# An attention kernel's last six exps made whole again, its jitter seeds redrawn

## The chip, the cores and the metric

One core of one Trainium2 chip runs the whole program. The metric is the device time of one execution in microseconds, the median over several runs. The profile is of one execution, and times inside it count from its first instruction.

## What is computed

The input `x` has 2,048 rows of 512 values. It is layer-normalised; the result feeds multi-query attention with 32 heads of 16 (one key and one value head) and a dense branch with a hidden width of 1,792; the two are multiplied and added to `x`.

```python
def _A_ref(x, wq, wk, wv, wo):
    B, S, D = x.shape
    H = 32
    Dh = D // H
    q = (lambda x, *d: x.transpose(*d))((x @ wq).reshape(B, S, H, Dh), 0, 2, 1, 3)
    k = x @ wk
    v = x @ wv
    scores = jnp.einsum("bhqd,bkd->bhqk", q, k) * (Dh ** -0.5)
    p = _softmax(scores, axis=-1)
    o = jnp.einsum("bhqk,bkd->bhqd", p, v)
    return (lambda x, *d: x.transpose(*d))(o, 0, 2, 1, 3).reshape(B, S, H * Dh) @ wo

def _B_ref(x, w1, w2):
    h = jnp.einsum("bsd,df->bsf", x, w1)
    h = _silu(h)
    out = jnp.einsum("bsf,fd->bsd", h, w2)
    return out

x = A_x
xn = _layernorm(x, axis=-1)
s = _A_ref(xn, A_wq, A_wk, A_wv, A_wo)
g = _silu(_B_ref(xn, B_w1, B_w2))
return x + s * g
```

## The kernel before

**Tiles.** Queries come in four chunks of 512 (`NQ`), heads in octets; a *group* is one chunk with the even or the odd heads of an octet, four heads in four row strips of TensorE, and there are `NG` = 32 groups. A group has 64 *scores*: four heads by sixteen key tiles of 128, each a matmul of 32 x 128 weights with 512 columns into one PSUM bank (L866). Seven banks (`BANKS`) serve scores and jobs, the eighth (`OB`) collects a group's products with V.

**Two ways to exponentiate.** Most scores go to ScalarE, which takes the exp of up to three banks in one instruction (L1717, into `pa_sb`). The others go to VectorE in *batches* of four, one for each head: one `tensor_scalar` writes a 16-bit pattern that reads as an approximate exponential (L1002, into `db_sb`), and three more copies of the whole batch with an integer added (`ds_sb`, "shifts") are made by GpSimd (L1202) or VectorE (L1196). Four such copies with four weighted versions of V make the approximation, so a VectorE score (a "D slot") costs four PV matmuls and a ScalarE score one. PV matmuls run as rounds of up to four, side by side in four column strips (L1282). `END_DV` lets VectorE take shifts in the last group once fewer than that many of its scores are left; `MARGIN_END` is the number of scores that must be left in the last group for a new batch to start (`d_batch`).

**Jobs.** Rounds of the projections and of the dense branch (`q`, `h`, `z`, `w`; L511) fill TensorE between score phases.

**The order.** No order is written by hand. A planner (`Planner`, and the `*_step` functions) walks through modelled time at build time, always for the engine that is furthest behind, and appends what that engine does next; semaphore waits come from the dependences. The order on each engine is then fixed. `do_S` places a *score phase* of up to four scores and decides how many go to VectorE: with four free banks two, with three one, or two when fewer than about ten PV matmuls are queued for the two open groups (`held`: a job holds a bank; Q3 = QUEUE = 10, Q4 = -1, J3 = N3 = 1, J4 = N4 = 2). A backlog of VectorE tasks (`dve_backlog`, which counts a shift only while `END_DV` lets VectorE take it) lowers this to one or none:

```python
queue = sum(len(q) for g in range(st["gO"], min(st["gO"] + 2, NG)) for q in pvq[g])
...
if held:
    want = J4 + (queue < vary(Q4)) if n == 4 else J3 + (queue < vary(Q3))
else:
    want = N4 if n == 4 else max(N3, 2 * (queue < vary(QUEUE)))
```

`vary` multiplies a threshold by a random factor of width `SPREAD`; the generator gets the next of `SEEDS` every `STRETCH` = 64 phases.

**The end.** When at most `RH` = 6 ScalarE scores are left, `begin_halves` and `half_step` take their exps by halves of 256 queries (L1667), first all first halves, then all second halves. PV rounds follow by halves, and `last_norm` is called once for each half: transpose of the PV sums (`f_sb`, L1306), reciprocal (L1309), multiplication (L1311), transpose back (`on_sb`, L1316). `make_tail` sets up the output projection of the last four row tiles (four `wo` rounds each, the last of which needs `on_sb`), as soon as no job is left (`MT_EARLY`). `scaled` multiplies its result by the gate: for row tiles 0 and 2 (`EVR`) ScalarE copies the bank to SBUF (L714) and VectorE multiplies from there (L716); tiles 1 and 3 are multiplied straight from PSUM (L719). Tiles 0 to 2 are added to `x` by TensorE (L1503) and copied out by ScalarE (L1508), tile 3 by VectorE (L731). SyncE issues the stores (L725).

Of the kernel before, what the change touches and what calls it, by code (L numbers as in the profile page):

```python
# [15 lines left out]
P = 128  # L16
DH = 16
# [4 lines left out]
SEEDS, STRETCH, SPREAD = (2502, 4652, 1398, 4134, 3319, 6151, 8548, 1413, 942, 5642), 64, 0.3  # L22
# [30 lines left out]
MARGIN, MARGIN_END = 16, 20  # L53
# [15 lines left out]
END_DV = 40  # L69
RH, EVR, SC_PRIO, MT_EARLY = 6, (0, 2), 0, 1  # L70
# [225 lines left out]
def bass_recurrent_scan__grouped_kv_mqa__dense_activation_silu__prompt_kernel(  # L296
# [30 lines left out]
    with ExitStack() as es:  # L327
# [383 lines left out]
        def scaled(tt, b, r=None):  # L711
            k = tt % 2
            if r in EVR:
                ev = pl.add(Task(AC, 490.0, lambda a: a.activation(xn_sb[:, r, :], bank(b), ACT.Copy, scale=0.25),  # L714
                                 [("ps", b)], [("xn", r)], 0))
                fin_task[tt] = Task(DV, 333.0, lambda v: v.tensor_tensor(fin_sb[:, k, :], xn_sb[:, r, :], tmp_sb[:, tt % 8, :], ALU.mult),  # L716
                                    [("xn", r), ("tmp", tt % 8)], [("fin", k)], SC_PRIO, [ev, tmp_task[tt], fin_task.get(tt - 2)], ports=2)
                return fin_task[tt]
            fin_task[tt] = Task(DV, T_P, lambda v: v.scalar_tensor_tensor(  # L719
                out=fin_sb[:, k, :], in0=bank(b), scalar=0.25, in1=tmp_sb[:, tt % 8, :], op0=ALU.mult, op1=ALU.mult),  # L720
                [("ps", b), ("tmp", tt % 8)], [("fin", k)], 0 if r is None else SC_PRIO, [tmp_task[tt], fin_task.get(tt - 2)])
            return fin_task[tt]
# [92 lines left out]
        st = dict(half=0, halfdone=False, half1=[0] * 4, gA=0, gD=0, gO=0, fill=0, expn=0, assigned=0)  # L815
# [179 lines left out]
        def pass_d(b, bt, g, i, kt):  # L995
            tot[g, i] += K

            def placed(pop):
                pool_free.append(b)
                pvq[g][i].append((pop, v_lhs(1, g, kt), db_sb[:, bt.b, i * NQ:(i + 1) * NQ].bitcast(BF16),  # L1000
                                  [("Db", bt.b, i)] + v_reads(1, kt), ("d", bt), None))
            bt.P[i] = pl.add(Task(DV, T_P, lambda v: v.tensor_scalar(  # L1002
                db_sb[:, bt.b, i * NQ:(i + 1) * NQ], bank(b), 128.0 * LOG2E, 128.0 * (SHIFT_BETA + 127.0),
                op0=ALU.mult, op1=ALU.add), [("ps", b)], [("Db", bt.b, i)], 0, on_place=placed))
# [163 lines left out]
        def split(bt, s, j):  # L1168
# [3 lines left out]
            def ready(pop, slots):  # L1172
                for i in slots:
# [3 lines left out]
                                         [("Ds", s, i)] + v_reads(j, kt), ("s", s), None))  # L1177
# [38 lines left out]
        def pv_round(t):  # L1216
# [9 lines left out]
            liked = "a" if ap >= PA_HI else "s" if ap <= DS_HI and all(ds_busy) else "ads"  # L1226
            soon, old = INF, INF
            for half in ((None, 0, 1) if st["half"] else (None,)):
                got = {}
                if half == 1 and (st["half"] < 2 or last_t1[0].op is None):  # L1230
                    break
                for i in range(4):
                    pick = None
                    for k, ent in enumerate(pvq[g][i]):
                        if ent[5] != half:
                            continue
                        if v_task.get(ent[3][-1][2]) is None or v_task[ent[3][-1][2]].op is None:
                            continue
                        r = max(pl.vis(ent[0], PE), pl.ready(PE, ent[3], ()))
                        if r <= t + 20:  # L1240
                            key = (ent[4][0] not in liked, k)
                            if pick is None or key < pick[0]:
                                pick = (key, k, r)
                            if key[0] is False:
                                break
                            continue
                        if pick is None:
                            soon = min(soon, r)
                    if pick is not None:
                        got[i] = pick[1]  # L1250
                        old = min(old, pick[2])
                if got:
                    break
# [6 lines left out]
        def do_pv(t, got):  # L1260
# [3 lines left out]
            for i in sorted(got):  # L1264
                ent = pvq[g][i].pop(got[i])
                op_, lhs, rhs, rd, rel, half = ent
# [10 lines left out]
            cols = slice(0, NQ) if half is None else slice(half * NQ // 2, (half + 1) * NQ // 2)  # L1277

            def emit(pe, mm=tuple(mm)):
                h = None  # L1280
                for (i, lhs, rhs, s0, s1) in mm:
                    h = pe.matmul(bank(OB)[32 * i:32 * (i + 1), cols], lhsT=lhs, rhs=rhs, start=s0, stop=s1,  # L1282
                                  tile_position=(0, 32 * i), skip_group_check=True)
                return h
            pl.place(PE, MM if half is None else MM / 2, emit, sorted(reads, key=str), [("ps", OB)], t0=max(t, pe_start(pl.clk[PE], "C")))
            pl.set_mode("C")
            make_shifts()
            if st["half"] == 1 and not any(e[5] != 1 for q in pvq[g] for e in q) and st["halfdone"] and all(
                    tot[g, i] - done[g, i] == st["half1"][i] for i in range(4)):
                last_norm(g, 0)  # L1290
# [4 lines left out]
        def last_norm(g, h):  # L1295
            oi, e = divmod(g, 2)
            k = g % 2
            f3 = f_sb[:, k, :].rearrange("p (b d) -> p b d", d=32)
            o3 = otr_sb[:, oi % 2, :].rearrange("p (b d) -> p b d", d=32)
            den = DH if e == 0 else 0  # L1300
            val = 0 if e == 0 else DH
            nb = NQ // 64
            cols = slice(h * NQ // 2, (h + 1) * NQ // 2)
            bl = slice(h * nb, (h + 1) * nb)
            late = last_t1[-1:] if h else [norm.get(("m", g - 2))]
            t1 = pl.add(Task(DV, 0.5 * T_TR + 30.0, lambda v: v.transpose(f_sb[:, k, cols], bank(OB)[:, cols]),  # L1306
                             [("ps", OB)], [("F", k, h)] + [("F", k)] * (h == 0), 1 + h, late))
            last_t1.append(t1)
            t2 = pl.add(Task(DV, 110.0, lambda v: v.reciprocal(rcp_sb[:, k, bl], f3[:, bl, den]),  # L1309
                             [("F", k, h)], [("rcp", k, h)], 3, [t1]))  # L1310
            t3 = pl.add(Task(DV, 200.0, lambda v: v.tensor_tensor(  # L1311
                o3[:, bl, val:val + DH], f3[:, bl, val:val + DH],
                rcp_sb[:, k, bl].unsqueeze(2).to_broadcast([P, nb, DH]), ALU.mult),
                [("F", k, h), ("rcp", k, h)], [("otr", oi % 2, 1, h)] + [("otr", oi % 2, 1)] * (h == 0), 3,
                [t2, t2_task.get(oi - 2)], ports=2))
            last_on.append(pl.add(Task(DV, 0.5 * T_TR + 30.0, lambda v: v.transpose(  # L1316
                on_sb[:, oi % NON, cols], otr_sb[:, oi % 2, cols]),
                [("otr", oi % 2, 0), ("otr", oi % 2, 1, h)], [("on", oi % NON, h)] + [("on", oi % NON)] * (h == 0), 4 + h,
                [t3, norm[("m", g - 1)]] + last_on)))
            if h:  # L1320
                norm[g] = t1
            st["half"] = 2 + h

        last_t1 = []
        last_on = []

        def make_norm(g):
# [6 lines left out]
            if g == NG - 1:  # L1334
                for h in range(len(last_t1), 2):
                    last_norm(g, h)
                return
# [112 lines left out]
        tb = []  # L1450
        tail = dict(made=False, items=[], sums=[])

        def make_tail():
            tail["made"] = True
            c = NC - 1
            free = sorted((pl.ready(PE, (), [("ps", b)]), b) for b in pool_free)
            held = [u.bank for u in units[st["expn"]:]]
            tb.extend([b for _, b in free] + held)
            assert sorted(tb) == list(BANKS), tb
            for r in range(4):  # L1460
                tt = 4 * c + r
                for o in range(NOC):
                    def emit(pe, r=r, o=o):
                        return col4(pe, tb[r], lambda j: on_sb[:, (NOC * c + o) % NON, r * P + 32 * j:r * P + 32 * (j + 1)],
# [9 lines left out]
        def tail_round(t):  # L1474
            soon = INF
            for n, (_, r, o, emit) in enumerate(tail["items"][:1]):
# [5 lines left out]
                rr = pl.ready(PE, tail_reads(r, o), [("ps", tb[r])]) if tb[r] in pool_free else INF  # L1482
# [3 lines left out]
            for n, (r, part) in enumerate(tail["sums"]):  # L1486
# [5 lines left out]
                rr = pl.ready(PE, [("fin", tt % 2)] if part else [("xr", tt % 4)], () if part else [("ps", tb[4 + r])]) if tb[4 + r] in pool_free else INF  # L1492
# [5 lines left out]
        def do_tail(t, it):  # L1498
            if it[0] == "s":
# [3 lines left out]
                pl.place(PE, MM, lambda pe: pe.matmul(bank(tb[4 + r]), lhsT=ident[:, :], rhs=src, start=part == 0, stop=part == 1),  # L1503
                         [("fin", tt % 2) if part else ("xr", tt % 4)] + [("id", i) for i in range(4)], [("ps", tb[4 + r])],
                         t0=max(t, pe_start(pl.clk[PE], "F")))
                pl.set_mode("F")
                if part:
                    t2 = pl.add(Task(AC, 490.0, lambda a: a.activation(ob_sb[:, tt % 4, :], bank(tb[4 + r]), ACT.Copy),  # L1508
                                     [("ps", tb[4 + r])], [("ob", tt % 4)], 0, [out_task.get(tt - 4)]))
# [3 lines left out]
            pl.place(PE, MM, emit, tail_reads(r, o), [("ps", tb[r])], t0=max(t, pe_start(pl.clk[PE], "C")))  # L1513
            pl.set_mode("C")
            if o == NOC - 1:
                tt = 4 * (NC - 1) + r
                if r < 3:
                    stt[r] = pl.add(scaled(tt, tb[r], r))
                else:
                    for tk in final(tt, tb[r]):  # L1520
# [299 lines left out]
```

## Time and profile before

| what | value |
|---|---|
| median of 4 runs | 669.73 us (669.61 to 670.07) |
| the profiled execution | 670.07 us |
| its span, first to last instruction | 668.3 us |
| busy: PE, ACT, DVE, POOL | 98%, 98%, 92%, 84% |
| score matmuls; to VectorE | 2,048; 736 |
| shifts by GpSimd; by VectorE | 544; 8 |
| exps by ScalarE, whole; by halves | 671; 6 |

PE is TensorE's matmuls, PEld its weight loads, DVE VectorE, ACT ScalarE, POOL GpSimd and SP SyncE. L1282 is line 1282 of the kernel; a line of the timeline gives the start and the duration in us, engine, line, operation, output and input, how many, and in brackets the idle time before and what ended it. A matmul's own duration is longer than the time that it keeps TensorE from the next one, so costs are taken from starts.

### The profile page before, as it was taken

How to read it: one execution, taken by the hardware profiler on the slowest of the kernel's cores; microseconds unless marked ns; L12 is line 12 of the kernel's file. 1: busy time of each engine (PE TensorE's matmuls, PEld its weight loads, DVE VectorE, ACT ScalarE, POOL GpSimd, SP SyncE). 2: the span in 40 equal slices, each digit the busy share in tenths (PEclk: the TensorE clock that was granted, in tenths of full speed). 3: DMA queues.
4: the chain of work that ended last, by engine and by line, in shares of the span. 5: the costliest groups of instructions: out<-in, count | busy, mean ns of one | idle time of the engine just before them, and what ended most of it. 6: DMA issues, size and time to landing. Idle time of an engine off the chain costs nothing.

```text
span 668.3 us, 21224 instructions
## 1 busy us (share of the span) xinstructions
PE 656.9 (98%) x8963; PEld 190.9 (29%) x8963; DVE 614.9 (92%) x1093; ACT 652.0 (98%) x768; POOL 558.8 (84%) x556
## 2 busy tenths in 40 slices
PE   7999999999999999999999999999999999999997
PEld 4422222222222222222222222222222222222223
DVE  8989999899989998999998999999899999998995
ACT  6999999999999999999999999999999999999996
POOL 3049889989898899898899887999899989998972
PEclk9999999999999999999999999999999999999999
DMA  9500000000000000000000000000000000000000
GB/s 292 174 9 2 2 2 2 2 3 1 2 2 18 19 18 18 1 2 2 2 2 2 17 18 18 18 2 1 3 2 2 2 18 17 18 18 2 2 2 33
DMA packets 11821, 12.86 MB, mean 19 GB/s; under 512 B 1808, under 2 KB 11216, under 8 KB 11728
## 3 DMA queue, kind: packets, MB, share of 16 engines
q1 hardware_dynamic: 10928, 10.78, 5.1%
q8 instruction: 72, 1.18, 0.8%
q10 hardware_dynamic: 800, 0.72, 0.3%
q14 instruction: 21, 0.17, 0.1%
HBM read 8.95 MB, written 2.10 MB: 17 GB/s over the span
## 4 chain that ended last, share of the span: by engine, by line
PE 75%; ACT 17%; DVE 5%; DMA 1%; issue 0%; SPq 0%; ACTq 0%
PE ps L1282 33%; PE ps L866 25%; PE ps L511 17%; ACT pa_sb L1717 16%; DVE db_sb L1002 1%; ACT t_sb L669 1%; DVE stats_sb L458 1%; DMA ds_sb<-in_A_x_dram 1%; DVE u_sb L671 1%; DVE xn_sb L487 0%; DVE xnT_sb L538 0%; SPq L393 0%; DVE fin_sb L719 0%; DVE kt_sb L567 0%; DVE mv_sb L462 0%
## 5 line engine op out<-in xcount | busy, mean ns | idle before, releaser
L1202 POOL INT64_ADD ds_sb<-db_sb x544 | 553.1, 1038 | 91.8 <-DVE db_sb L1002 35.2
L1717 ACT ACTIVATE pa_sb<-ps 128x1024 bf16<-128x1024 f32 (+2 forms) x671 | 616.3, 1029 | 5.8 <-PE ps L866 3.4
L1002 DVE TENSOR_SCALAR db_sb<-ps 128x512 uint16<-128x512 f32 x736 | 475.0, 682 | 39.8 <-PE ps L866 28.9
L1282 PE MATMUL ps<-ds_sb,v_sb 128*32 128x512 bf16 x2208 | 274.4, 383 | 0.0
L866 PE MATMUL ps<-qt_sb,kt_sb 32*128 32x512 bf16 x2048 | 250.7, 384 | 3.7 <-ACT pa_sb L1717 1.1
L1282 PE MATMUL ps<-pa_sb,v_sb 128*32 128x512 bf16 x1317 | 245.8, 382 | 0.0
L1282 PE MATMUL ps<-db_sb,v_sb 128*32 128x512 bf16 x736 | 176.2, 383 | 0.0
L866 PEld LDWEIGHTS ps<-qt_sb,kt_sb 32*128 32x128 bf16 x2048 | 62.6, 90 | 275.5 <-ACT pa_sb L1717 154.5
L1282 PEld LDWEIGHTS ps<-ds_sb,v_sb 128*32 128x32 bf16 x2208 | 68.4, 95 | 60.4 <-issue 41.9
L511 PE MATMUL ps<-xnT_sb,w_sb 128*32 128x512 bf16 x896 | 72.0, 384 | 0.0
L1282 PEld LDWEIGHTS ps<-pa_sb,v_sb 128*32 128x32 bf16 x1317 | 60.7, 95 | 39.3 <-issue 26.7
L511 PE MATMUL ps<-w_sb,u_sb 128*32 128x512 bf16 x820 | 64.2, 384 | 0.0
L1282 PEld LDWEIGHTS ps<-db_sb,v_sb 128*32 128x32 bf16 x736 | 43.7, 95 | 20.3 <-issue 15.9
L669 ACT ACTIVATE t_sb<-ps 128x512 bf16<-128x512 f32 x72 | 45.2, 628 | 0.0
L671 DVE SCALAR_TENSOR_TENSOR u_sb<-t_sb,ps 128x512 bf16<-128x512 bf16 x56 | 38.3, 684 | 1.4
L618 PE MATMUL ps<-w_sb,u_sb 32*128 32x512 bf16 x76 | 29.2, 384 | 0.0
L511 PEld LDWEIGHTS ps<-xnT_sb,w_sb 128*32 128x32 bf16 x896 | 17.2, 94 | 27.3 <-issue 21.5
L511 PEld LDWEIGHTS ps<-w_sb,u_sb 128*32 128x32 bf16 x820 | 15.4, 95 | 23.0 <-issue 19.7
L1338 DVE STREAM_TRANSPOSE f_sb<-ps 128x512 f32<-128x512 f32 x31 | 21.9, 706 | 0.1
L511 PE MATMUL ps<-wo_sb,on_sb 128*32 128x512 bf16 x256 | 19.8, 383 | 0.0
L511 PE MATMUL ps<-xnT_sb,wq_sb 128*32 128x512 bf16 x240 | 18.8, 384 | 0.0
L1342 DVE TENSOR_TENSOR otr_sb<-f_sb,rcp_sb 128x256 bf16<-128x256 f32 x31 | 12.9, 416 | 1.4 <-POOL ds_sb L1202 1.1
(75 smaller groups left out, 167.7 us busy)
## 6 DMA issues: line engine op xcount, KB each, us to landing
w_sb<-in_B_w_dram SPq DMA_DIRECT2D x2, 1792.0 KB, 14.4
xr_sb<-in_A_x_dram SPq DMA_DIRECT2D x16, 128.0 KB, 2.9
out_dram<-ob_sb SPq DMA_DIRECT2D x16, 128.0 KB, 1.7
ds_sb<-in_A_x_dram SPq DMA_DIRECT2D x3, 512.0 KB, 7.5
wq_sb<-in_A_wq_dram SPq DMA_DIRECT2D x1, 512.0 KB, 5.6
wo_sb<-in_A_wo_dram SPq DMA_DIRECT2D x1, 512.0 KB, 16.2
kt_sb<-kt_sb ACTq DMA_DIRECT2D x4, 112.0 KB, 3.9
ds_sb<-in_A_x_dram ACTq DMA_DIRECT2D x2, 128.0 KB, 3.0
```

The lines of the kernel that those rows point to most:

```text
L458: ts_ = pl.add(Task(DV, 593.0, lambda v, t=t: v.bn_stats(stats_sb[:, t, :], x_tile(t)), [xkey(t)], [("st", t)], 1 + j, gate=(lambda j=j: S ...
L511: last = h.matmul(bank(b)[32 * j:32 * (j + 1), 0:n], lhsT=lhs(j), rhs=rhs, start=start, stop=stop, tile_position=(0, 32 * j), skip_group_c ...
L618: return (lambda pe: pe.matmul(bank(b), lhsT=lhs(k, rows, 0, P), rhs=rhs(k, rows), start=False, stop=last, tile_position=(32 * i, 0), skip ...
L669: t1 = Task(AC, 490.0, lambda a: a.activation(t_sb[:, k, :], src, ACT.Tanh, scale=scale), [held], [("t", k)], 0, [t0])
L671: t2 = Task(DV, T_P, lambda v: v.scalar_tensor_tensor(out=dst, in0=t_sb[:, k, :], scalar=1.0, in1=src, op0=ALU.add, op1=ALU.mult), [held, ...
L866: return pe.matmul(bank(b), lhsT=kt_sb[32 * i:32 * i + 32, g % 2, kt * P:(kt + 1) * P], rhs=qt_sb[32 * i:32 * i + 32, (g // 2) % NQR, :], ...
L1002: bt.P[i] = pl.add(Task(DV, T_P, lambda v: v.tensor_scalar(db_sb[:, bt.b, i * NQ:(i + 1) * NQ], bank(b), 128.0 * LOG2E, 128.0 * (SHIFT_BET ...
L1202: whole["po"].append(pl.add(Task(PO, T_P64, lambda g, cols=cols: g.int64_add(ds_sb[:, s, cols].bitcast(U64), db_sb[:, bt.b, cols].bitcast( ...
L1282: h = pe.matmul(bank(OB)[32 * i:32 * (i + 1), cols], lhsT=lhs, rhs=rhs, start=s0, stop=s1, tile_position=(0, 32 * i), skip_group_check=True)
L1338: t1 = pl.add(Task(DV, T_TR, lambda v: v.transpose(f_sb[:, k, :], bank(OB)), [("ps", OB)], [("F", k)], 1, [norm.get(("m", g - 2))]))
L1342: t3 = pl.add(Task(DV, 332.0, lambda v: v.tensor_tensor(o3[:, :, val:val + DH], f3[:, :, val:val + DH], rcp_sb[:, k, :].unsqueeze(2).to_br ...
L1717: op = pl.place(AC, 0.8333 * NQ * n + T_AF, lambda a: a.activation(pa_sb[:, s * NQ:(s + n) * NQ].rearrange("p (b n) -> p b n", n=NQ), ps3[ ...
```

## The change

The half-width end goes: the last exps are as wide as all others, the last PV rounds are whole, and `last_norm` runs once, after the last PV round, with its four steps two by two. `make_tail` waits until every exp is placed and uses banks in numerical order instead of by when they come free. Tiles 0 and 2 are multiplied from PSUM like tile 1. `MARGIN_END` goes from 20 to 28, `END_DV` from 40 to 0 (VectorE makes no shifts). The ten seeds become six others, so that the sixth stays from phase 320 on, and `SPREAD` falls from 0.3 to 0.2. The queue rule of `do_S` above is the same line in both.

```diff
-SEEDS, STRETCH, SPREAD = (2502, 4652, 1398, 4134, 3319, 6151, 8548, 1413, 942, 5642), 64, 0.3
+SEEDS, STRETCH, SPREAD = (1020, 3123, 1104, 3421, 6268, 3265), 64, 0.2
...
-MARGIN, MARGIN_END = 16, 20
+MARGIN, MARGIN_END = 16, 28
...
-END_DV = 40
-RH, EVR, SC_PRIO, MT_EARLY = 6, (0, 2), 0, 1
+END_DV = 0
...
-        def scaled(tt, b, r=None):
+        def scaled(tt, b):
             k = tt % 2
-            if r in EVR:
-                ev = pl.add(Task(AC, 490.0, lambda a: a.activation(xn_sb[:, r, :], bank(b), ACT.Copy, scale=0.25),
-                                 [("ps", b)], [("xn", r)], 0))
-                fin_task[tt] = Task(DV, 333.0, lambda v: v.tensor_tensor(fin_sb[:, k, :], xn_sb[:, r, :], tmp_sb[:, tt % 8, :], ALU.mult),
-                                    [("xn", r), ("tmp", tt % 8)], [("fin", k)], SC_PRIO, [ev, tmp_task[tt], fin_task.get(tt - 2)], ports=2)
-                return fin_task[tt]
             fin_task[tt] = Task(DV, T_P, lambda v: v.scalar_tensor_tensor(
                 out=fin_sb[:, k, :], in0=bank(b), scalar=0.25, in1=tmp_sb[:, tt % 8, :], op0=ALU.mult, op1=ALU.mult),
-                [("ps", b), ("tmp", tt % 8)], [("fin", k)], 0 if r is None else SC_PRIO, [tmp_task[tt], fin_task.get(tt - 2)])
+                [("ps", b), ("tmp", tt % 8)], [("fin", k)], 0, [tmp_task[tt], fin_task.get(tt - 2)])
...
-            for half in ((None, 0, 1) if st["half"] else (None,)):
-                got = {}
-                if half == 1 and (st["half"] < 2 or last_t1[0].op is None):
-                    break
-                for i in range(4):
-                    pick = None
-                    for k, ent in enumerate(pvq[g][i]):
-                        if ent[5] != half:
...
-            pl.place(PE, MM if half is None else MM / 2, emit, sorted(reads, key=str), [("ps", OB)], t0=max(t, pe_start(pl.clk[PE], "C")))
+            pl.place(PE, MM, emit, sorted(reads, key=str), [("ps", OB)], t0=max(t, pe_start(pl.clk[PE], "C")))
             pl.set_mode("C")
             make_shifts()
-            if st["half"] == 1 and not any(e[5] != 1 for q in pvq[g] for e in q) and st["halfdone"] and all(
-                    tot[g, i] - done[g, i] == st["half1"][i] for i in range(4)):
-                last_norm(g, 0)
...
-        def last_norm(g, h):
-            oi, e = divmod(g, 2)
-            k = g % 2
-            f3 = f_sb[:, k, :].rearrange("p (b d) -> p b d", d=32)
-            o3 = otr_sb[:, oi % 2, :].rearrange("p (b d) -> p b d", d=32)
-            den = DH if e == 0 else 0
-            val = 0 if e == 0 else DH
+        def last_norm(g, oi, k, f3, o3, den, val):
             nb = NQ // 64
-            cols = slice(h * NQ // 2, (h + 1) * NQ // 2)
-            bl = slice(h * nb, (h + 1) * nb)
-            late = last_t1[-1:] if h else [norm.get(("m", g - 2))]
-            t1 = pl.add(Task(DV, 0.5 * T_TR + 30.0, lambda v: v.transpose(f_sb[:, k, cols], bank(OB)[:, cols]),
-                             [("ps", OB)], [("F", k, h)] + [("F", k)] * (h == 0), 1 + h, late))
-            last_t1.append(t1)
-            t2 = pl.add(Task(DV, 110.0, lambda v: v.reciprocal(rcp_sb[:, k, bl], f3[:, bl, den]),
-                             [("F", k, h)], [("rcp", k, h)], 3, [t1]))
-            t3 = pl.add(Task(DV, 200.0, lambda v: v.tensor_tensor(
-                o3[:, bl, val:val + DH], f3[:, bl, val:val + DH],
-                rcp_sb[:, k, bl].unsqueeze(2).to_broadcast([P, nb, DH]), ALU.mult),
-                [("F", k, h), ("rcp", k, h)], [("otr", oi % 2, 1, h)] + [("otr", oi % 2, 1)] * (h == 0), 3,
-                [t2, t2_task.get(oi - 2)], ports=2))
-            last_on.append(pl.add(Task(DV, 0.5 * T_TR + 30.0, lambda v: v.transpose(
-                on_sb[:, oi % NON, cols], otr_sb[:, oi % 2, cols]),
-                [("otr", oi % 2, 0), ("otr", oi % 2, 1, h)], [("on", oi % NON, h)] + [("on", oi % NON)] * (h == 0), 4 + h,
-                [t3, norm[("m", g - 1)]] + last_on)))
-            if h:
-                norm[g] = t1
-            st["half"] = 2 + h
-
-        last_t1 = []
+            t1, t2, t3 = [], [], []
+            for h in range(2):
+                cols = slice(h * NQ // 2, (h + 1) * NQ // 2)
+                t1.append(pl.add(Task(DV, 0.5 * T_TR + 30.0, lambda v, cols=cols: v.transpose(f_sb[:, k, cols], bank(OB)[:, cols]),
+                                      [("ps", OB)], [("F", k, h)] + [("F", k)] * (h == 0), 1 + h, [norm.get(("m", g - 2))] + t1)))
+            for h in range(2):
+                bl = slice(h * nb, (h + 1) * nb)
+                t2.append(pl.add(Task(DV, 110.0, lambda v, bl=bl: v.reciprocal(rcp_sb[:, k, bl], f3[:, bl, den]),
+                                      [("F", k, h)], [("rcp", k, h)], 3, [t1[1], t1[h]])))
+            for h in range(2):
+                bl = slice(h * nb, (h + 1) * nb)
+                t3.append(pl.add(Task(DV, 200.0, lambda v, bl=bl: v.tensor_tensor(
+                    o3[:, bl, val:val + DH], f3[:, bl, val:val + DH],
+                    rcp_sb[:, k, bl].unsqueeze(2).to_broadcast([P, nb, DH]), ALU.mult),
+                    [("F", k, h), ("rcp", k, h)], [("otr", oi % 2, 1, h)] + [("otr", oi % 2, 1)] * (h == 0), 3,
+                    [t2[1], t2[h], t2_task.get(oi - 2)] + t3, ports=2)))
+            for h in range(2):
+                cols = slice(h * NQ // 2, (h + 1) * NQ // 2)
+                last_on.append(pl.add(Task(DV, 0.5 * T_TR + 30.0, lambda v, cols=cols: v.transpose(
+                    on_sb[:, oi % NON, cols], otr_sb[:, oi % 2, cols]),
+                    [("otr", oi % 2, 0), ("otr", oi % 2, 1, h)], [("on", oi % NON, h)] + [("on", oi % NON)] * (h == 0), 4 + h,
+                    [t3[1], t3[h], norm[("m", g - 1)]] + last_on)))
+            norm[g] = t1[1]
...
-                for h in range(len(last_t1), 2):
-                    last_norm(g, h)
-                return
+                return last_norm(g, oi, k, f3, o3, den, val)
...
-            free = sorted((pl.ready(PE, (), [("ps", b)]), b) for b in pool_free)
-            held = [u.bank for u in units[st["expn"]:]]
-            tb.extend([b for _, b in free] + held)
-            assert sorted(tb) == list(BANKS), tb
...
-                        return col4(pe, tb[r], lambda j: on_sb[:, (NOC * c + o) % NON, r * P + 32 * j:r * P + 32 * (j + 1)],
+                        return col4(pe, r, lambda j: on_sb[:, (NOC * c + o) % NON, r * P + 32 * j:r * P + 32 * (j + 1)],
...
-                    stt[r] = pl.add(scaled(tt, tb[r], r))
+                    stt[r] = pl.add(scaled(tt, r))
                 else:
-                    for tk in final(tt, tb[r]):
+                    for tk in final(tt, r):
...
-            if st["assigned"] == NG * SLOTS and (MT_EARLY and not active and st["job"] == len(jobs) or st["expn"] == len(units)) and not tail["made"] and all(
+            if st["assigned"] == NG * SLOTS and st["expn"] == len(units) and not tail["made"] and all(
...
-        def begin_halves():
-            rest = units[st["expn"]:]
-            ops = []
-            while rest:
-                q = rest[:2]
-                if len(q) > 1 and abs(q[1].bank - q[0].bank) != 1:
-                    q = q[:1]
-                rest = rest[len(q):]
-                s = next(k for k in range(NPA - len(q) + 1) if not any(pa_busy[k:k + len(q)]))
-                for d, u in enumerate(sorted(q, key=lambda u: u.bank)):
-                    pa_busy[s + d] = 1
-                    tot[u.slot[0], u.slot[1]] += 1
-                    st["half1"][u.slot[1]] += 1
-                ops.append((sorted(q, key=lambda u: u.bank), s))
-            halves.extend([(q, s, h) for h in range(2) for q, s in ops])
-            st["half"] = 1
...
-            cols = slice(h * NQ // 2, (h + 1) * NQ // 2)
-            b0 = q[0].bank
-            op = pl.place(AC, 0.8333 * NQ / 2 * n + T_AF, lambda a: a.activation(
-                pa_sb[:, s * NQ:(s + n) * NQ].rearrange("p (b n) -> p b n", n=NQ)[:, :, cols], ps3[:, b0:b0 + n, cols], ACT.Exp),
-                [("ps", u.bank) for u in q], [("pA", s + d, h) for d in range(n)] + [("pA", s + d) for d in range(n) if h == 0])
-            for d, u in enumerate(q):
-                g, i, kt = u.slot
-                if h:
-                    pool_free.append(u.bank)
-                    st["expn"] += 1
-                pvq[g][i].append((op, v_lhs(0, g, kt), pa_sb[:, (s + d) * NQ + h * NQ // 2:(s + d) * NQ + (h + 1) * NQ // 2],
-                                  [("pA", s + d, h)] + v_reads(0, kt), ("a", s + d), h))
...
-            if not st["half"] and st["assigned"] == NG * SLOTS and 0 < len(units) - st["expn"] <= RH and all(
-                    u.slot[0] == NG - 1 for u in units[st["expn"]:]):
-                begin_halves()
-            if halves:
-                return half_step(t)
```

## The prediction

> **What bounds the kernel now.** The page comes first: which engines are full.
>
> ```profile
> span 668.3 us, 21224 instructions
> ...
> PE 656.9 (98%) x8963; PEld 190.9 (29%) x8963; DVE 614.9 (92%) x1093; ACT 652.0 (98%) x768; POOL 558.8 (84%) x556
> ...
> PE 75%; ACT 17%; DVE 5%; DMA 1%; issue 0%; SPq 0%; ACTq 0%
> ```
>
> TensorE and ScalarE are both at 98%, and the chain that ended last runs over TensorE for three quarters of the span. The windows say where this holds.
>
> ```profile
> 640.00:650.00 10.00, 9.96 (x149) 3.04 (x145) 9.73 (x18) 9.84 (x13) 6.41 (x7) 1.00 0.02 3
> 650.00:658.00 8.00, 8.00 (x124) 2.53 (x120) 6.17 (x10) 8.00 (x12) 4.16 (x5) 1.00 0.00 1
> 658.00:662.40 4.40, 4.40 (x81) 2.60 (x78) 2.67 (x9) 2.67 (x7) 0.00 (x0) 1.00 0.02 4
> 662.40:668.30 5.90, 2.31 (x14) 0.52 (x13) 2.33 (x5) 2.50 (x5) 0.00 (x0) 0.84 0.25 89
> ```
>
> Columns: stretch, length, then busy time of PE, PEld, DVE, ACT, POOL. Up to 658 us PE and ACT have no room; in the last 10 us nobody is full and the end is a chain of small steps. So the body is priced as throughput, the end as a chain. The chain in order of time gives the body's prices:
>
> ```profile
> 647.92 0.22 PE ps L511 x4
> ...
> 651.94 0.98 PE ps L1282 x16
> 652.91 0.33 PE ps L866 x4
> ```
>
> A round of four column matmuls costs 0.22 us (0.216 from start to start). Four PV rounds and one score phase take 0.98 + 0.33 = 1.31 us, so a phase costs 1.31 - 4 x 0.22 = 0.43, with three matmuls in it or with four. Counted in the trace there are 640 phases for 2,048 scores, 736 of them for VectorE. A VectorE score needs four PV matmuls instead of one: 3/4 of a round, 0.16 us of PE. It saves ScalarE 0.46, half of the 0.92 between the two-bank exp at 655.89 and the next at 656.81.
>
> The timelines of ACT, DVE and SP give the end:
>
> ```profile
> 657.77 2.64 ACT L1667 ACTIVATE pa_sb<-ps 128x512 bf16<-128x512 f32 x6
> 659.53 0.45 DVE L1306 STREAM_TRANSPOSE f_sb<-ps 128x256 f32<-128x256 f32 x1 [1.70 <-PE ps L1282]
> 660.57 0.45 DVE L1316 STREAM_TRANSPOSE on_sb<-otr_sb 128x256 bf16<-128x256 bf16 x1
> 660.94 0.41 DVE L1306 STREAM_TRANSPOSE f_sb<-ps 128x256 f32<-128x256 f32 x1
> 661.95 0.45 DVE L1316 STREAM_TRANSPOSE on_sb<-otr_sb 128x256 bf16<-128x256 bf16 x1
> 662.14 0.60 ACT L714 ACTIVATE xn_sb<-ps 128x512 bf16<-128x512 f32 x1 [1.73 <-PE ps L511]
> 662.35 0.69 DVE L719 SCALAR_TENSOR_TENSOR fin_sb<-ps,tmp_sb 128x512 bf16<-128x512 f32 x1
> 664.60 1.81 SPq L725 DMA_DIRECT2D out_dram<-ob_sb  x4
> ```
>
> Half 0's normalisation starts at 659.53, while ScalarE is still exponentiating half 1 (until 660.41). From 659.53 to 662.39 VectorE runs the eight half operations without a stop. The first store is issued at 664.60, the other three follow at the queue's pace, and the span ends 3.7 us later.
>
> **Part 1: the end without halves: +1.0 us (0.6 to 1.5).** Times are those of the profile of before, as if all up to the last score phase stayed.
> - Exps: the five last score tiles go in 0.92 + 0.92 + 0.48 = 2.32 us plus 0.1 of latency instead of 2.64, so they end at 660.2. A single-bank exp keeps its engine for 0.48 (656.81 to 657.29).
> - The last PV round starts 0.12 later, as now (660.41 to 660.53), takes 0.39, and the transpose follows 0.14 after: 660.85 for the first `f_sb`. Half 0 thus starts 1.3 us later than at 659.53.
> - New order: both `f_sb`, both reciprocals, both multiplies, both `on_sb`, each pair waiting for the pair before. Back to back a half transpose takes 0.37 (660.57 to 660.94): 660.85 + 0.37 + 0.43 = 661.65 first reciprocal; + 0.13 + 0.23 = 662.0 first multiply; + 0.22 + 0.32 = 662.55 first `on_sb`, done at 663.0 and the second at 663.37. Now these are done at 661.02 and 662.39: +2.0 and +1.0.
> - `wo` round for r = 0 at 663.18, read 0.5 later: 663.69. Four multiplications from PSUM at 0.61 each (662.35 to 662.96): the first ends at 664.38, the fourth at 666.2. Now row 0 passes ScalarE (0.60) and a 0.41 multiplication that queues behind row 1's 0.69, and ends at 663.38: +1.0 for the first store. The fourth row's addition (0.42) is done at 666.6, before SP's turn for the fourth store (665.60 + 1.36), so the pace of the stores, 1.81 for four, stays. +1.0.
> - `make_tail` comes later, when every exp is placed. Its twelve early `wo` rounds (12 x 0.216 = 2.6 us) then run from about 660.2 to 662.8, under VectorE's eight operations, which last to 663.18 for PE. If that cover is gone, each late round costs 0.22. High end: two of these and a little more, 1.5; low end: the exps in one three-bank group and an overlap of the pairs, 0.6.
>
> The page Perfetto Trace Analysis of the Trainium skill, section Optimizing Scalar/DVE Operations, speaks on both sides: grouping helps a saturated engine (about 51 ns a ScalarE instruction on PSUM), while breaking up lets others start sooner when the engine causes bubbles. By its first half alone this part would gain an estimated 0.15 us (three instructions fewer); by the row of `f_sb` it loses, since ScalarE is the engine that VectorE waits for here.
>
> **Part 2: MARGIN_END 20 to 28: +0.7 us (0 to 1.84).** The last VectorE batch now starts in the phase at 651.54, when 21 scores are left, and its four evictions run at 651.99, 653.29, 654.60 and 655.21. With 28 it may not start; the one before it begins with 30 or more left and stays. Four scores move to ScalarE: 4 x 0.46 = 1.84 us for an engine that is full up to its last exp; PE gets three PV rounds back (0.65), which helps nobody, because its queue is dry at 658.4. Against this stands `END_DV`: from 645.85 to 648.86 VectorE makes five shifts and no eviction, and waiting shifts count as backlog, which keeps `do_S` from giving it scores. Without them these 3.0 us hold five evictions at 0.6, and the four scores may be taken earlier, at 0. But the phases there have three banks, one eviction each unless the queue is short. I take 0.7, nearer to the end that the freed time speaks for.
>
> **Part 3: the shifts themselves, END_DV 40 to 0: nothing.** Eight leave VectorE (0.69 each). The five at 645.9 to 648.9 go to GpSimd at 1.04. GpSimd is idle from 645.45 to 649.04 and from 650.1 to 651.3, 4.8 us for 5.2 us of work; its last shift moves from 655.4 to about 656, and PE has older PV work until 658. Without this cover a late shift costs up to 1.0.
>
> **Part 4: six seeds, spread 0.2: +0.4 us (-1.3 to +2.3).** The slot rule itself (fewer than ten queued) stands on both sides. New random factors reorder every phase after the start, without a direction that a trace could show. Windows of 64 us of the score matmuls alone (PE, PEld):
>
> ```profile
> 208.00:272.00 64.00, 24.67 (x196) 6.14 (x196) 1.00 0.07 19
> 272.00:336.00 64.00, 26.26 (x220) 6.56 (x220) 1.00 0.01 2
> ```
>
> and the same windows of the VectorE evictions:
>
> ```profile
> 208.00:272.00 64.00, 45.67 (x71) 1.00 0.07 19
> 272.00:336.00 64.00, 53.48 (x84) 1.00 0.01 2
> ```
>
> More scores come with more VectorE scores, so the PE time saved in phases goes back into PV rounds. Three phases fewer at the same split give -3 x 0.43 = -1.3; five VectorE scores fewer cost ScalarE 5 x 0.46 = +2.3. With both engines at 98% a shift either way loses on one of them, hence +0.4 rather than 0.
>
> The same page's section Identifying the Most-Contended Engine judges TensorE by its weight loads, not by matmul time. PEld is at 29%, so by it phases would be free and only ScalarE's slots would count; part 4 would keep the 2.3 and lose the -1.3. The starts of rounds 0.216 us apart say that PE has no gaps, and I go by them.
>
> **Sum.** 1.0 + 0.7 + 0 + 0.4 = 2.1 us on the profiled execution (670.07 us, span 668.3), so 672.2; the median of the runs is 669.73, 0.34 lower: 671.8. About 0.2% (1.34 us) is what a measurement of this kernel can tell from no change: 668.4 to 671.1 counts as same.
>
> **Rivals.**
> - *The body absorbs the end* (0.21): part 2 is 0 and the redraw saves a phase or so (-0.5), with part 1 at 1.0: 670.2, no change. For it: VectorE's freed 3.0 us. Against: ACT at 8.00 of 8.00 us before 658.
> - *Redraw wins* (0.08): the new order packs the scores in fewer phases at an equal split. Its price is 0.43 a phase; against parts 1 and 2 (1.7) and the bound (1.3) it decides from eight phases fewer (632 instead of 640): 669.73 + 1.7 - 3.4 = 668.0. For it: 512 of 640 phases hold only three scores. Against: the two windows above, where more scores came with more VectorE work.
> - *Redraw loses* (0.11, on the forecast's side): five VectorE scores fewer, +2.3 in place of +0.4: 673.7.
> - *The named rule does nothing* is sure as far as the rule goes: it is the same line in both, so no time is given to it.
>
> **How the numbers follow.** Slower by over 0.2%: 0.60 for the forecast and 0.11 for the lost redraw, 0.71; same 0.21; faster 0.08. The high end takes all high bounds, 1.5 + 1.84 + 2.3 = 5.6: 675.4. The low end takes part 1 at 0.6, part 2 at 0 and half of the redraw's gain (-0.7): 669.6.
>
> **What would show it.** Right: no half-width exps; two `f_sb` transposes back to back after the last PV round, the first `on_sb` done 2.1 us after the first of them starts, and the first store 4.7 us after that start; GpSimd shifts at 552 or thereabouts, none on VectorE; evictions in place of the five shifts at 646 to 649, and no batch begun in the last 27 scores. Wrong: phases below 632, or a number of VectorE scores above 740 with the exps ending earlier; an end from first `f_sb` to the first store under 4.2 us would refute part 1.

## The result and the profile after

The changed kernel takes 670.47 us (median of 33 runs, 670.36 to 670.81); before took 669.72 in the same comparison (53 runs). The ratio is 1.0011, with a 95% interval of 1.0007 to 1.0016: 0.75 us slower, clear of the scatter and within the 0.2% that the prediction called no change. The profiled execution of the changed kernel took 670.39 us, with a span of 668.6. That of before took 670.07, at the upper end of its runs, so the two spans stand only 0.3 apart; differences below go by the medians.

The page of the changed kernel, the lines that answer to those of before:

```profile
span 668.6 us, 21201 instructions
...
PE 658.6 (99%) x8958; PEld 190.6 (29%) x8958; DVE 609.3 (91%) x1085; ACT 650.7 (97%) x761; POOL 566.8 (85%) x564
...
PE 62%; ACT 30%; DVE 6%; issue 1%; DMA 0%; ACTq 0%
```

The same two engines are full. Counted in the trace, there are 641 phases instead of 640, and again 736 VectorE scores: the body does the same work. The windows of the end:

```profile
640.00:650.00 10.00, 10.00 (x144) 2.84 (x145) 8.59 (x15) 10.00 (x12) 9.09 (x10) 1.00 0.01 3
650.00:658.00 8.00, 8.00 (x123) 2.53 (x112) 0.69 (x1) 8.00 (x11) 8.00 (x9) 1.00 0.01 2
658.00:662.40 4.40, 4.30 (x75) 1.97 (x76) 2.08 (x8) 1.37 (x3) 1.30 (x2) 1.00 0.00 0
```

Between 650 and 658 us VectorE (third) falls from 6.17 to 0.69, and GpSimd (fifth) rises from 4.16 to 8.00 and goes on past 658. The timelines of POOL, ACT, DVE and SP of the changed kernel:

```profile
647.11 12.18 POOL L1195 INT64_ADD ds_sb<-db_sb  x12 [0.91 <-DVE otr_sb L1317]
656.84 2.53 ACT L1635 ACTIVATE pa_sb<-ps 128x1024 bf16<-128x1024 f32 x4
660.07 0.78 DVE L1281 STREAM_TRANSPOSE f_sb<-ps 128x256 f32<-128x256 f32 x2 [6.53 <-PE ps L1266]
661.38 0.77 DVE L1296 STREAM_TRANSPOSE on_sb<-otr_sb 128x256 bf16<-128x256 bf16 x2
662.44 2.61 DVE L712 SCALAR_TENSOR_TENSOR fin_sb<-ps,tmp_sb 128x512 bf16<-128x512 f32 x4 [0.30 <-PE ps L510]
664.68 2.05 SPq L718 DMA_DIRECT2D out_dram<-ob_sb  x4
```

GpSimd runs twelve shifts without a stop until 659.3. Before, its last four ended at 655.38 and VectorE's last three at 657.82:

```profile
651.30 4.08 POOL L1202 INT64_ADD ds_sb<-db_sb  x4 [1.22 <-PE ps L1282]
655.92 1.90 DVE L1196 TENSOR_SCALAR ds_sb<-db_sb 128x2048 uint16<-128x2048 uint16 x3
```

The last exp of the changed kernel ends 0.1 after its last shift, at 659.37 (before 660.41), and the first `f_sb` transpose starts at 660.07. From there the end has the form that the prediction drew: transposes in pairs, four multiplications from PSUM, first store 4.61 us after the first transpose. In these two executions the exps end 1.04 us earlier, and the chain behind them is longer, 5.31 us to the first store instead of 4.19. Of the 1.04, 0.48 was there before the end began: with 64 scores left the changed kernel stood at 636.07 and before at 636.55.

### The profile page after: what moved, and what is told of

It is laid out like the page before. It is cut to its first block, busy times and chain, and to the rows that moved or that the text cites. A ratio compares the mean times of both kernels' runs of the same rounds, so it can differ in the third digit from the quotient of the medians.

```text
span 668.6 us, 21201 instructions
## 1 busy us (share of the span) xinstructions
PE 658.6 (99%) x8958; PEld 190.6 (29%) x8958; DVE 609.3 (91%) x1085; ACT 650.7 (97%) x761; POOL 566.8 (85%) x564
## 4 chain that ended last, share of the span: by engine, by line
PE 62%; ACT 30%; DVE 6%; issue 1%; DMA 0%; ACTq 0%
ACT pa_sb L1635 29%; PE ps L1266 27%; PE ps L859 21%; PE ps L510 14%; ACT t_sb L668 2%; DVE stats_sb L457 1%; DVE db_sb L995 1%; DVE u_sb L670 1%; DVE xnT_sb L537 0%; DVE xn_sb L486 0%; DMA ds_sb<-in_A_x_dram 0%; DVE fin_sb L712 0%; DVE mv_sb L461 0%; DVE kt_sb L566 0%; PE ps L526 0%
## 5 line engine op out<-in xcount | busy, mean ns | idle before, releaser
L1195 POOL INT64_ADD ds_sb<-db_sb x552 | 561.1, 1038 | 87.8 <-DVE db_sb L995 34.9
L617 PE MATMUL ps<-w_sb,u_sb 32*128 32x512 bf16 x80 | 30.8, 385 | 0.0
L670 DVE SCALAR_TENSOR_TENSOR tmp_sb<-t_sb,ps 128x512 bf16<-128x512 bf16 x16 | 11.0, 687 | 4.5 <-ACT t_sb L668 3.7
```

Source lines behind the costliest of these rows:

```text
L617: return (lambda pe: pe.matmul(bank(b), lhsT=lhs(k, rows, 0, P), rhs=rhs(k, rows), start=False, stop=last, tile_position=(32 * i, 0), skip ...
L670: t2 = Task(DV, T_P, lambda v: v.scalar_tensor_tensor(out=dst, in0=t_sb[:, k, :], scalar=1.0, in1=src, op0=ALU.add, op1=ALU.mult), [held, ...
L1195: whole["po"].append(pl.add(Task(PO, T_P64, lambda g, cols=cols: g.int64_add(ds_sb[:, s, cols].bitcast(U64), db_sb[:, bt.b, cols].bitcast( ...
```

## The experiments

Theory A is the prediction's sum: end, last group and redraw each cost their own, and the costs add. Theory B: the body (seeds and last group) gets faster and absorbs part of the end. Theory C: the new end is nearly free. After the first four runs two more were opposed: G, that GpSimd's last shift holds the end in the changed last group, and M, that `MARGIN_END` costs. Differences are medians against before as run beside them (669.80 to 669.83).

| run | what differs from before | us | difference | ratio (95%) |
|---|---|---|---|---|
| the change | all | 670.47 | +0.75 | 1.0011 (1.0007 to 1.0016) |
| `e1_end_only` | new end | 670.77 | +0.96 | 1.0014 (1.0006 to 1.0023) |
| `e2_seeds_only` | new seeds, spread 0.2 | 669.88 | +0.07 | 1.0001 (0.9993 to 1.0010) |
| `e3_group_only` | `MARGIN_END` 28, `END_DV` 0 | 670.46 | +0.65 | 1.0010 (1.0001 to 1.0019) |
| `e4_all_but_end` | the last two together | 670.38 | +0.57 | 1.0008 (0.9999 to 1.0017) |
| `e5_shifts_back` | new seeds, `MARGIN_END` 28 | 671.28 | +1.45 | 1.0022 (1.0014 to 1.0031) |
| `e6_shifts_off` | `END_DV` 0 | 670.33 | +0.50 | 1.0008 (0.9999 to 1.0016) |
| `e7_margin_only` | `MARGIN_END` 28 | 671.44 | +1.61 | 1.0024 (1.0014 to 1.0034) |
| `e8_no_halves` | `RH` = 0 | 670.45 | +0.62 | 1.0009 (1.0001 to 1.0018) |
| `e9_open_late_old` | `MARGIN_END` 28, `END_DV` 20 | 670.47 | +0.67 | 1.0011 (1.0002 to 1.0020) |
| `e10_open_late_new` | the same, new seeds | 670.33 | +0.53 | 1.0008 (0.9999 to 1.0017) |
| `e11_draw_p` | the change with other seeds | 673.52 | +3.72 | 1.0056 (1.0043 to 1.0068) |
| `e12_draw_q` | the change with other seeds | 673.78 | +3.98 | 1.0060 (1.0047 to 1.0072) |

The intervals are some 0.6 us to each side, and those of `e4`, `e6` and `e10` still hold 1. But where the order on the engines turned out to be the same, medians agree within 0.14 us, and in every experiment from +0.50 up the fastest execution is slower than the slowest of before beside it. So differences below 0.14 are read as none, those of 0.5 and more as real.

### One part at a time

`e1_end_only`, the changed kernel with these lines as before:

```diff
-SEEDS, STRETCH, SPREAD = (1020, 3123, 1104, 3421, 6268, 3265), 64, 0.2
+SEEDS, STRETCH, SPREAD = (2502, 4652, 1398, 4134, 3319, 6151, 8548, 1413, 942, 5642), 64, 0.3
-MARGIN, MARGIN_END = 16, 28
+MARGIN, MARGIN_END = 16, 20
-END_DV = 0
+END_DV = 40
```

> The changed kernel with the seeds, spread, MARGIN_END and END_DV of before: only the end differs from before. Theory A (the terms of the prediction): the whole end costs 1.0, so 670.7 us, first f_sb about 0.5 to 1.3 later than before and the first store 1.0 later. Theory B (the body absorbed part of the end): the same +1.0 or a little more, 670.7 to 670.9, with 5.3 us instead of 4.2 from the end of the last exp to the first store. Theory C (the new end is nearly free, the body did not change): at most +0.3, 669.7 to 670.0.

Measured: +0.96. Theory C falls; A and B both allow it. Its DVE timeline:

```profile
660.49 0.78 DVE L1281 STREAM_TRANSPOSE f_sb<-ps 128x256 f32<-128x256 f32 x2 [2.87 <-PE ps L1266]
662.86 2.61 DVE L712 SCALAR_TENSOR_TENSOR fin_sb<-ps,tmp_sb 128x512 bf16<-128x512 f32 x4 [0.30 <-PE ps L510]
```

First transpose 660.49 against 659.53 before; the first store 4.61 later at 665.10, against 664.60. Its body, which is that of before, ran 0.2 us earlier in this execution (with 64 scores left it stood at 636.34, before at 636.55), so on one clock the first transpose is 1.2 later and the first store 0.7. The remaining 0.24 is the pace of the four stores, 2.05 us instead of 1.81.

`e2_seeds_only`, before with the new line of seeds:

```diff
-SEEDS, STRETCH, SPREAD = (2502, 4652, 1398, 4134, 3319, 6151, 8548, 1413, 942, 5642), 64, 0.3
+SEEDS, STRETCH, SPREAD = (1020, 3123, 1104, 3421, 6268, 3265), 64, 0.2
```

> Before with the six new seeds and spread 0.2, nothing else. Theory A: +0.4, 670.1 us. Theory B: faster by about 0.5, 669.2 us, because with 64 scores left the changed kernel stood at 636.07 and before at 636.55. Theory C: 669.7 us, no change.

Measured: +0.07, no change that these runs can tell. Theory B rested on 636.07 against 636.55 with 64 scores left. The other profiles put that in its place: kernels with the old seeds stand anywhere from 636.16 to 636.55 at that point, those with the new from 636.07 to 636.56. The change and `e10_open_late_new` (below) have the same order on every engine up to 657 us, and stood at 636.07 and 636.56. So the 0.5 us is the scatter of two executions.

`e3_group_only`:

```diff
-MARGIN, MARGIN_END = 16, 20
+MARGIN, MARGIN_END = 16, 28
-END_DV = 40
+END_DV = 0
```

> Before with MARGIN_END 28 and END_DV 0, nothing else: the last group alone is planned otherwise. Theory A: four scores more for ScalarE in part, +0.7, 670.4 us, 732 VectorE scores. Theory B: the freed VectorE takes the four scores earlier, 736 VectorE scores, last exp no later, 669.4 to 669.8 us.

Measured: +0.65. Theory A's number with theory B's mechanism: still 736 VectorE scores. What is late is told below. `e4_all_but_end` has these edits and the seeds of the run before:

> Before with the new seeds, spread, MARGIN_END and END_DV, and the old half-width end. Theory A: 0.4 + 0.7 = +1.1, 670.8 us. Theory B: -0.3 to -0.8, 668.9 to 669.4 us, faster than both kernels.

Measured: +0.57, the 0.07 and the 0.65 within the scatter. So the body did not get faster, and B falls as well. But A does not hold either: 0.96 + 0.07 + 0.65 = 1.68, and the change costs 0.75. The new end costs 0.96 on the body of before and 0.75 - 0.57 = 0.18 on the new one.

### Why the new end is cheap on the new last group

The DVE and POOL timelines of `e4_all_but_end`, which still has the halves:

```profile
660.05 0.45 DVE L1306 STREAM_TRANSPOSE f_sb<-ps 128x256 f32<-128x256 f32 x1 [6.42 <-PE ps L1282]
656.32 3.06 POOL L1202 INT64_ADD ds_sb<-db_sb  x3
```

Half 0 starts at 660.05 here and at 660.07 in the changed kernel, which has no halves. Half 0 may be normalised only after every other PV matmul of the group. The last PV matmul of the first halves of the exps starts at 658.86, but GpSimd's last shift, which ends at 659.38, still has its PV round to come (starts 659.52 to 659.63). Ending the first halves of the exps early buys nothing ahead of it.

The four kernels on one clock, in us from the start of the score phase with 64 scores left (636.55, 636.34, 636.15 and 636.07 in their profiles):

| kernel | last shift ends | last exp ends | first `f_sb` | first store | fourth store |
|---|---|---|---|---|---|
| before | 21.27 | 23.86 | 22.98 | 28.05 | 29.41 |
| `e1_end_only` | 21.27 | 23.67 | 24.15 | 28.76 | 30.36 |
| `e4_all_but_end` | 23.23 | 23.49 | 23.90 | 28.60 | 29.95 |
| the change | 23.23 | 23.30 | 24.00 | 28.61 | 30.21 |

On this clock `e4_all_but_end` and `e10_open_late_new`, which have one order, give the same 23.90 and 28.60. From before to `e1_end_only` the first transpose moves by 1.17 us, from `e4_all_but_end` to the change by 0.10. There the first store stays where it was (28.60 and 28.61); the 0.26 by which the fourth is later is the pace of the stores. So what the new end still costs on the new last group is that pace, and the halves themselves are worth nothing there. Between the upper two rows and the lower two the seeds change together with the last group; the new end with the new last group and the old seeds was not run.

`e2_seeds_only` is the contrast. There, too, GpSimd makes the last shifts, but ends them at 22.46 on this clock; their PV round starts (658.82 in its profile) before the last PV matmul of the first halves (659.12), the first transpose follows at 23.15, and the run loses nothing.

Theory G says that the shift holds half 0, and the next three runs took the two edits of the last group apart.

`e6_shifts_off` (`END_DV = 0` alone):

> Before with END_DV 0 alone, MARGIN_END still 20. Theory G: +0.6 or more, since a batch that starts later is shifted by GpSimd alone: 670.4 to 671.3 us, first f_sb after GpSimd's last shift. Theory M: 669.8 us, as before.

Measured: +0.50, and in the POOL, PE and DVE timelines

```profile
649.26 10.16 POOL L1202 INT64_ADD ds_sb<-db_sb  x10
659.13 0.90 PE L511 MATMUL ps<-wo_sb,on_sb 128*32 128x512 bf16 x12
659.77 0.47 PE L1282 MATMUL ps<-ds_sb,v_sb 128*32 128x512 bf16 x4
660.29 0.45 DVE L1306 STREAM_TRANSPOSE f_sb<-ps 128x256 f32<-128x256 f32 x1 [7.23 <-PE ps L1282]
```

the last shift at 659.42 again. The lines of TensorE show how the shift holds half 0. Its PV round starts 0.35 us after it (0.14 in `e4_all_but_end`), behind twelve matmuls with `wo`, and TensorE is not idle between 650 us and the end of that round. The planner puts `wo` rounds there only while no PV round is ready in its modelled time (`pe_step`). So it is the planned order that waited for the shift; on the chip the round waits for its turn on TensorE, and a shift that ended sooner under the same order would not move it.

The order of `e6_shifts_off` on every engine is the same as that of `e3_group_only`: with `END_DV` 0, `MARGIN_END` 20 or 28 changes no instruction. The two are one program, and 670.33 and 670.46 show how far a median repeats.

`e7_margin_only` (`MARGIN_END = 28` alone):

> Before with MARGIN_END 28 alone, END_DV still 40. Theory G: 669.6 to 669.9 us, no change, last shift on VectorE. Theory M, and part 2 of the prediction: 732 VectorE scores, four more for ScalarE, +0.4 to +0.7, 670.2 to 670.5 us.

Measured: +1.61. This is the mechanism of the prediction's part 2, at nearly its full price of 1.84: 732 VectorE scores, and ScalarE late. The group in the page, and the line of the ACT timeline:

```profile
L1002 DVE TENSOR_SCALAR db_sb<-ps 128x512 uint16<-128x512 f32 x732 | 472.4, 682 | 38.5 <-PE ps L866 27.4
```

```profile
659.12 2.86 ACT L1667 ACTIVATE pa_sb<-ps 128x512 bf16<-128x512 f32 x6
```

The half exps begin at 659.12 instead of 657.77. G's number for this run was missed, since it counted only shifts, and M's was too low.

`e5_shifts_back`, which is `e4_all_but_end` with

```diff
-END_DV = 0
+END_DV = 40
```

> The run of all changes but the end, with END_DV back at 40: VectorE may make shifts in the last group again. Theory G (what the last group costs is GpSimd's last shift, which ends at 659.4 and holds back the round of PV after which half 0 may be normalised): last shift of any engine before 658.5, first f_sb about 659.3 to 659.5 instead of 660.05, 669.6 to 669.9 us instead of 670.38. Theory M (MARGIN_END 28 costs it, by fewer or earlier batches): no gain, 670.3 to 670.5 us.

Measured: +1.45, a miss for both. It meant to free GpSimd, but waiting shifts count as VectorE's backlog again, so the batches come late, the last one is not begun, and it has 732 VectorE scores like `e7_margin_only`. `MARGIN_END` 28 is dear with `END_DV` 40 and costs nothing with 0.

`e9_open_late_old` and `e10_open_late_new` were to give VectorE only the late shifts, and to beat both kernels:

```diff
-MARGIN, MARGIN_END = 16, 20
+MARGIN, MARGIN_END = 16, 28
-END_DV = 40
+END_DV = 20
```

> Before with MARGIN_END 28 and END_DV 20: waiting shifts count as VectorE backlog, and VectorE may take them, only once fewer than 20 scores of the last group are left. If GpSimd's last shift (659.5 with END_DV 0) is what holds back half 0: VectorE, idle from 650 on, takes three to six shifts, the last shift ends before 657, still 736 VectorE scores, first f_sb 659.2 to 659.5 instead of 660.38, 669.4 to 669.9 us instead of 670.46. Rival (the last exps hold it as well): first f_sb no earlier than 660, 670.2 to 670.5 us.

> The same with the six new seeds and spread 0.2. If the shift held it: last exp 659.4 to 659.7 as in the run of all changes but the end, first f_sb 658.8 to 659.3 instead of 660.05, 669.2 to 669.7 us, below before by 0.1 to 0.6. Rival: 670.2 to 670.5 us.

Measured: +0.67 and +0.53. Nothing was tested: VectorE took no shift, and on every engine the order is that of `e3_group_only` and `e4_all_but_end`. They serve as repeats (670.46 and 670.47; 670.38 and 670.33). That GpSimd's last shift, through the planned order, holds half 0 therefore rests on the order of events in the profiles (two orders, five profiles) and on `e6_shifts_off`; taking it away without anything else was not achieved.

### What in the end costs

`e8_no_halves`:

```diff
-RH, EVR, SC_PRIO, MT_EARLY = 6, (0, 2), 0, 1
+RH, EVR, SC_PRIO, MT_EARLY = 0, (0, 2), 0, 1
```

> Before with RH = 0 alone: the last exps whole, the rest of the old end (copies of tiles 0 and 2 by ScalarE, early set-up of the tail) kept; the two halves of the last normalisation still run one after the other, half 0 first. If whole exps are what the new end costs on this body (+1.0 in the end-only run): first f_sb at 660.4 to 660.7 and about +0.9, 670.7 us. If the copies or the early set-up carry a good part: +0.4 to +0.6, 670.3 us.

Measured: +0.62, nearer to the second. Of the 0.96 of the whole new end it makes some two thirds. The DVE and SP timelines:

```profile
660.32 0.78 DVE L1306 STREAM_TRANSPOSE f_sb<-ps 128x256 f32<-128x256 f32 x2 [2.88 <-PE ps L1282]
664.91 1.81 SPq L725 DMA_DIRECT2D out_dram<-ob_sb  x4
```

The transposes go in pairs (x2) here too, not one half after the other as was expected, so the 0.62 holds the new order of the normalisation as well as the whole exps. From first transpose to first store it takes 4.59, as good as the 4.61 of the new end; but its four stores are issued in 1.81, those of the new end in 2.05. So the ScalarE copies of tiles 0 and 2, with the early set-up, do not bring the first store forward. VectorE, which has two shorter multiplications for them, finishes tile 3's addition 2.3 us after its first multiplication starts instead of 2.95, in time for the second store. That is 0.24 of the remaining 0.34; the other 0.1 is within the scatter. Copies and early set-up were not taken apart.

### Two draws that nobody chose

`e11_draw_p` and `e12_draw_q` are the changed kernel with other seeds:

```diff
-SEEDS, STRETCH, SPREAD = (1020, 3123, 1104, 3421, 6268, 3265), 64, 0.2
+SEEDS, STRETCH, SPREAD = (7412, 9172, 7630, 7403, 8321, 9624), 64, 0.2
...
+SEEDS, STRETCH, SPREAD = (3112, 3026, 8388, 7795, 3051, 1543), 64, 0.2
```

> The changed kernel with six other seeds, drawn at random and not chosen. The prediction's bounds for a redraw are -1.3 to +2.3 around its own middle. If a redraw is worth little: 670.0 to 671.2 us. If the order matters by phases and the split: up to 672.8 us, with the difference readable as phases x 0.43 and as moved VectorE scores x 0.46.

> The same with a second random draw of six seeds: 670.0 to 671.2 us if a redraw is worth little, up to 672.8 us if not.

Measured: 673.52 and 673.78, 3.1 and 3.3 above the change and beyond every bound. Neither phases (642 and 639, against 641) nor VectorE scores (736 and 740) explain it. One window over the body, first of the changed kernel,

```profile
40.00:640.00 600.00, 598.57 (x8098) 166.34 (x8098) 560.00 (x933) 596.79 (x687) 542.43 (x534) 1.00 0.03 7
```

then of `e11_draw_p`:

```profile
40.00:640.00 600.00, 596.39 (x8056) 165.52 (x8057) 557.29 (x928) 595.68 (x683) 539.95 (x532) 1.00 0.03 7
```

TensorE is idle for 3.6 us instead of 1.4. That is 2.2 of the 2.4 us by which the draw is late, give or take the scatter of a start, when 64 scores are left (638.50 against 636.07). In `e12_draw_q` it is 1.6 of 2.8 (596.94 busy), and four VectorE scores more make 4 x 0.16 = 0.65; what the rest is stays open. Not all of the 3.1 and 3.3 lies in the profile: between the span and the device time stand 2.2 and 2.1 us in the draws, 1.8 in the change and in before. What takes these 0.3 to 0.4 us more stays open.

## Why the prediction was right and wrong

The range held the time. The likeliest case, slower by over 0.2%, did not come; the measured 670.47 lies by the rival in which the body absorbs the end, 670.2. That is luck for the most part: of the rival's terms only part 2 at nothing came true, while its redraw (-0.5) measured +0.07, its end (1.0) came to 0.18 on this last group, and the shifts, which it puts at nothing, cost 0.50.

- **Part 1, the end, +1.0:** right on the body it was worked out for (`e1_end_only`, +0.96), but not in its pieces: the first store was to come 1.0 later at an unchanged pace, and came 0.7 later with 0.24 more for the pace. Within it, in the changed kernel, the first transpose to the first store was put at 4.75 and took 4.61; the first `on_sb` was done 1.75 after the first transpose instead of 2.15, because reciprocals start 0.11 apart and the multiplies begin while they still run. The time won there was lost again in TensorE's queue, where three matmuls of `x` stand before the sum of tile 0: `fin_sb` was done at 663.13 and its matmul started at 663.64. The pace of the stores, said to stay at 1.81, became 2.05.
- **Part 2, `MARGIN_END`, +0.7 (0 to 1.84):** both ends were real, one for each setting of `END_DV`: +1.61 with 40, and nothing with 0, which is the case of the change. The reason given for the low end, that the freed VectorE takes the four scores earlier, is in the trace: evictions at 645.08, 645.66, 646.93 and 647.55 where the shifts were. The value between them described neither.
- **Part 3, the shifts, nothing:** the step that failed in kind. It costs +0.50 alone. GpSimd's last shift was put at about 656 and ended at 659.3 to 659.5. The count was five shifts moved and three gone with the lost batch; but part 2's own low end keeps that batch, so its three shifts go to GpSimd too, and the earlier batches come faster than 1.01 us a shift can follow: twelve in a row in 12.18 us.
- **Part 4, the redraw, +0.4 (-1.3 to +2.3):** +0.07 for the seeds of the change. The bound was worked out in the wrong currency: two other draws cost 3.1 and 3.3 us more than these, at almost the same phases and split, mainly by TensorE waiting. The part sets the starts of TensorE's rounds against the weight-load share alone; the section that it cites (the Trainium skill, Perfetto Trace Analysis, Identifying the Most-Contended Engine) asks for the share of the peak matmul rate (MFU) as well, which was not worked out.
- **The sum, +2.1:** measured one by one, the parts are 0.96 + 0.65 + 0.07 = 1.68. The change costs 0.75. The step that failed is the addition: the halves only pay when the exps are the last thing that half 0 waits for. With the shifts late they no longer are, so the new end costs 0.18 instead of 0.96. In the terms of the prediction the 2.1 came to 0.18 + 0 + 0.50 + 0.07 = 0.75: three terms too high and one too low, so the range was held partly by errors that cancel.
- **The Trainium skill**, Perfetto Trace Analysis, section Optimizing Scalar/DVE Operations: it says that larger operations can raise the throughput of a saturated engine, and that breaking up instructions may let work end sooner where ScalarE or VectorE is not saturated but causes bubbles on other engines. Both effects are seen. Whole exps end 0.19 us sooner (23.67 against 23.86 in the table above), where the prediction estimated 0.15. Halved ones let VectorE start sooner where ScalarE is what it waits for (+0.62 without them), here on a ScalarE that is full up to its last exp. And they bring nothing where another input is later.

No version tried here beats before.

## What to carry to other kernels

Price two edits at the end of a kernel together whenever both move inputs of the same step: list every engine that the step waits for, with its last finish, and only the latest counts. Where one part of an estimate has a low end because work is done earlier by somebody, carry that work into the other parts' counts as well. And what an order is worth is shown by a draw that nobody chose: here two random draws cost about 3 us, four times the effect of the whole change. That both lines of seeds came out of a search is only inferred from this.

## What the runs showed that was not expected

An order with almost the same phases and the same split between engines can be 3 us slower in 670, and 2.2 us of it are waits of TensorE, none of which reaches 0.6 us. And one order stands up to 0.5 us apart in two executions: the body of before stood at 636.55, 636.34 and 636.16 us with 64 scores left in three profiles (before, `e1_end_only`, `e8_no_halves`), that of the change at 636.07 and 636.56 in two. Counted from that point, the first `f_sb` and the first store of one order repeat within 0.01 us.
